# Pairs of lots of 512 tokens instead of 416, seven plain chunks instead of eight, and ten operand buffers

## The chip, the core and the metric

The kernel runs on one core of one Trainium2 chip. The metric is device time in microseconds (us). In the views PE is the matmul engine (PEld its weight loads), DVE the vector engine, ACT the scalar engine, POOL the GpSimd engine and SP the engine that issues most DMAs. Each engine works through its own instructions in the order in which they were issued; semaphores order the engines against each other.

## The reference

The input is `x` of 8 batches, 3008 tokens, 256 channels: 24064 tokens in all. Two stages follow each other.

```
X = np.fft.rfft(x, axis=1)
Yr = Xr @ w_r - Xi @ w_i + b_r
Yi = Xr @ w_i + Xi @ w_r + b_i
Yr, Yi = soft threshold by 0.01
y = np.fft.irfft(Yr + 1j * Yi, n=3008, axis=1)
...
gate = 1.0 / (1.0 + np.exp(-(y @ w_gate)))
out = (gate * (y @ w_val)) @ w_out
```

`w_gate` and `w_val` are 256 x 1536, `w_out` is 1536 x 256. In the kernel the 1536 hidden channels are NF = 12 blocks of 128.

## The kernel before

**The transform stage.** The Fourier transform is made of matmuls with tables. `fwd_a` or `half_a` make its first factor and store to DRAM (`zd`), `fwd_b` the second, `mix` the products with `w_r` and `w_i`, `inv_b` and `inv_a` the way back (through `vd` in DRAM). Batches 0 and 1 are done nearly alone; batches 2 to 7 run as side work beside the plain chunks.

**Numbers in two parts.** A product of single precision is made of three matmuls: the operand is split in a high part (`hh`, `xh`, a cast on ACT) and a low part (`hl`, `xl`, a subtraction on DVE or POOL), and high x high, high x low and low x high are added in PSUM.

**Plain chunks.** The first NPL = 8 chunks of CW = 512 tokens go through `ffn1` and `ffn2`: for each of 12 blocks 12 matmuls of the first layer and 6 of the second, each of 512 columns, 216 matmuls a chunk. The side work is spread over the units of chunks 1 to 7 by weights. `SIDE_GAP` = 14 units at the end of the last chunk have none; there POOL, ACT and DVE also make sums of weights (`make_t`, `make_t1`) and the operands of the first pair.

**Pairs of lots.** The other 19968 tokens go in NPR = 24 pairs of two lots of HW = 416 tokens. A pair is a 2 x 2 block product in Winograd's form: seven products in place of eight. It has 12 half-steps, called e = 0 to 11 here, in `half(k, extra)` with k = 12 p + e for pair p. A half-step issues to PE: four products (banks a, b, d, c; operands a11, s2, s3, s1; 12 matmuls), then `second` (the output layer for an earlier block, 12 matmuls), then three products (bank a with operand a12, bank c with s4, bank d with a22; 9 matmuls). These are 33 matmuls of HW columns, 396 a pair. DVE adds the banks up (u, v, c12, tags `u`, `v`, `c`), ACT does sigmoids and high parts, DVE and POOL low parts. Even half-steps make gates, odd ones the products with them. The order is written out by hand here (`tc.manual_schedule()`): an engine's instructions run in the order of the code. Three lists hold what a half-step leaves to the next: `before_sums`, `after_m1` (run behind the first copy) and `before_second`. Through them, at the start of an even half-step, ACT makes the high parts of u and c12 and POOL the low part of c12.

**Operands.** `operand(p, name, sub_)` makes one of a pair's seven operands from the pair's tokens (`ypair`, loaded by `load_y`): for s1, s2, s3 and s4 a sum or difference on POOL, then for all a high part on ACT and a low part on POOL. The results lie in tiles of tag `xop`, NCB = 12 of them. In half-step e of pair p `extra()` makes those operands of pair p + 1 whose entry in `PREP_AT` is e; the call stands just ahead of `second`. `PREP` is (a11, s1, s2, s3, a12, s4, a22), `PREP_AT` (1, 3, 5, 7, 8, 11, 11).

**Outputs.** In half-step e = 2 `second` ends the pair before: four copies from PSUM to `ot` tiles (two on ACT, two on DVE, `bufs=4`), each followed by a store from SP.

Of the kernel before, what the change touches and what calls it, by code (L numbers as in the profile page):

```python
# [9 lines left out]
F32 = mybir.dt.float32  # L10
# [11 lines left out]
NQ = 2 * NK2  # L22
LAM = float(np.float32(0.01))
GROUPS = (1, 1, 2, 2, 2)
CW = 512
NPL = 8
HW = 416
FFT_BANKS, L1_BANKS, L2_BANKS = 3, 3, 2

NF2K, NR2K, NLD, NST, NBIG, NME, NVF, NHH, NSG, NYF = 5, 5, 3, 3, 5, 2, 3, 3, 2, 2  # L30
NCB, NTMP, NHP = 12, 9, 12

SIDE_GAP = 14
PRE = 4
# [2 lines left out]
NCONV = 6  # L37
# [69 lines left out]
def tile_fft_mix_ffn(ctx: ExitStack, tc, x, w_r, w_i, b_r, b_i, w_one, w_out, mf, mi, mis, fa, fa32, fb, out):  # L107
    nc = tc.nc
    B, S, D = x.shape
    P = 128  # L110
    CT = D // P
# [4 lines left out]
    UT = 2 * PT  # L116
    NU = B * H // 2
    T0 = NPL * CW
    NPR = (B * S - T0) // (2 * HW)
    assert T0 + NPR * 2 * HW == B * S  # L120
    NH = NF // 2
# [41 lines left out]
    def load_a(b, h):  # L163
        xf = p0.tile([P, 4, D], F32, name="xf0", bufs=R1 // 8) if b == 0 else big("xf")
        for lo_, hi_ in ((0, 64), (64, 2 * R2)):
            nc.sync.dma_start(xf[lo_:hi_], xv[b, lo_:hi_, 4 * h:4 * h + 4])
        held["x", b, h] = xf

    def product_a(xi, az, whole, copy):

        pa = bank("pa")[:2 * NQ]
        if whole:
            nc.tensor.matmul(pa, fa32_sb, xi, start=True, stop=True)
        else:
            xh = r2k("xh")[:2 * R2]
            xl = r2k("xl")[:2 * R2]
            nc.scalar.copy(xh, xi)
            nc.gpsimd.tensor_sub(xl, xi, xh)
            nc.tensor.matmul(pa, fa_sb[:, 0], xh, start=True, stop=False)
            nc.tensor.matmul(pa, fa_sb[:, 0], xl, start=False, stop=False)  # L180
            nc.tensor.matmul(pa, fa_sb[:, 1], xh, start=False, stop=True)
        copy(az, pa.rearrange("p (h c) -> p h c", h=2))

    def fwd_a(b, h, whole=False):
        xf = held.pop(("x", b, h))
        az = (p0.tile([P, 4, D], F32, name="az0", bufs=3) if b == 0 else big("az"))[:2 * NQ]
        for i in range(2):
            product_a(xf[:2 * R2, 2 * i:2 * i + 2], az[:, 2 * i:2 * i + 2], whole,
                      nc.vector.tensor_copy if b == 0 and i else nc.scalar.copy)
        nc.sync.dma_start(zv[b][:, 4 * h:4 * h + 4], az)  # L190
# [7 lines left out]
    def half_a(b, h, whole):  # L198

        xi = held.pop(("xh", b, h))[:2 * R2]  # L200
        az = p2.tile([P, 2, D], F32, tag="st", bufs=NST, name="azh")[:2 * NQ]
        product_a(xi, az, whole, nc.scalar.copy)
        nc.sync.dma_start(zv[b][:, 2 * h:2 * h + 2], az)


# [104 lines left out]


    def load_v(u):
        vf = p3.tile([P, 2, D], F32, name="vf", bufs=NVF)[:2 * NQ]
        b, h = divmod(2 * u, H)
        nc.sync.dma_start(vf, vv[b][:, h:h + 2])
        held["v", u] = vf
# [10 lines left out]
    def inv_a(u):  # L327
        vf = held.pop(("v", u))
        pa = bank("pia")[:, :CT * UT].rearrange("p (c h k) -> p c h k", c=CT, h=2)
        for hh in range(2):  # L330
            for ct in range(CT):
                nc.tensor.matmul(pa[:, ct, hh], vf[:, hh, ct * P:(ct + 1) * P], fb_sb[:, :PT], start=True, stop=True)  # L332
        py = pa.rearrange("p c h k -> p c (h k)")
        lo = u * UT
        n = 0
        if lo < T0:
            c, at = divmod(lo, CW)
            n = min(UT, CW - at)
            split_y(c, at, n, py[:, :, :n])
        if n == UT:  # L340
            return
        if lo + n < T0:
            t = p3.tile([P, CT, UT], F32, name="carry", bufs=1)[:, :, :UT - n]
            nc.scalar.copy(t, py[:, :, n:])
            held["carry", c + 1] = t, UT - n
        else:
            t = p3.tile([P, CT, UT], F32, name="yf", bufs=NYF)[:, :, :UT - n]
            nc.scalar.copy(t, py[:, :, n:])
            nc.sync.dma_start(yd[:, :, lo + n - T0:lo + UT - T0], t)

# [125 lines left out]

    def sums(fp, i):
        f0, f1 = 2 * fp, 2 * fp + 1
        b = p4.tile([P, 2, CT, P], F32, name="tb", bufs=1)
        nc.gpsimd.tensor_add(b, w1h[:, f0:f0 + 2, i], w1l[:, f0:f0 + 2, i])  # L480
        return b

    def make_t(fp, i):

        b = sums(fp, i)
        t = p4.tile([P, 3, P], F32, name="tt", bufs=1)
        g = nc.gpsimd
        g.tensor_sub(t[:, 1], b[:, 1, 1], b[:, 1, 0])
        g.tensor_add(t[:, 0], t[:, 1], b[:, 0, 0])
        g.tensor_sub(t[:, 2], b[:, 0, 1], t[:, 0])  # L490
        nc.scalar.copy(th[:, fp, i], t)
        sub(tl[:, fp, i], t, th[:, fp, i])

    def make_t1(fp, i):
        f0, f1 = 2 * fp, 2 * fp + 1
        b = p4.tile([P, 2, P], F32, name="tb1", bufs=1)
        nc.gpsimd.tensor_add(b, w1h[:, f0:f0 + 2, i, 0], w1l[:, f0:f0 + 2, i, 0])
        nc.gpsimd.tensor_sub(b[:, 1], b[:, 1], b[:, 0])
        nc.scalar.copy(w1h[:, f1, i, 0], b[:, 1])
        sub(w1l[:, f1, i, 0], b[:, 1], w1h[:, f1, i, 0])  # L500
# [39 lines left out]
        xs[p][name] = t  # L540

    PREP = ("a11", "s1", "s2", "s3", "a12", "s4", "a22")
    PREP_AT = (1, 3, 5, 7, 8, 11, 11)

    def tmp(name):
        return p5.tile([P, HW], F32, tag="tmp", bufs=NTMP, name=name)
# [17 lines left out]
    def second(n, j):  # L564

        if not 0 <= n < NPR * NH:
            return
        p, fp = divmod(n, NH)
        f = 2 * fp + j
        if f == 0:  # L570
            po[p] = [[bank("po", "l2", L2_BANKS)[:, :HW] for _ in range(CT)],
                     [psg.tile([P, 512], F32, tag="po2", bufs=CT, name="po2")[:, :HW] for _ in range(CT)]]
        for s in range(2):
            hh, hl = hq.pop((n, j, s))
            for ct in range(CT):
                o = po[p][s][ct]
                wh, wl = (w2[:, f, v, ct * P:(ct + 1) * P] for v in range(2))
                nc.tensor.matmul(o, wh, hh, start=(f == 0), stop=False)  # L578
                nc.tensor.matmul(o, wl, hh, start=False, stop=False)  # L579
                nc.tensor.matmul(o, wh, hl, start=False, stop=(f == NF - 1))  # L580
        if f == NF - 1:
            for s, os in enumerate(po.pop(p)):
                for ct, o in enumerate(os):
                    ot = p5.tile([P, HW], F32, name="ot2", bufs=4)
                    (nc.scalar.copy if ct == 0 else nc.vector.tensor_copy)(ot, o)  # L585
                    at = T0 + (2 * p + s) * HW
                    nc.sync.dma_start(out[ct * P:(ct + 1) * P, at:at + HW], ot)
# [20 lines left out]
    def half(k, extra):  # L608
# [32 lines left out]
            high(n, 1, 1, v)  # L641
            low(n, 1, 1, v, sub)
        run(before_second)
        if extra:
            extra()
        second(n - 1 - (i == 0), 1 - i)
        product(a, "a12", "b21", more=True)
        if i == 0:
# [94 lines left out]
    def load_part():  # L743
        k, f = parts.pop(0)
        raws.append((k, f, raw_words(w_out[f // 2] if k else w_one[f])))

    def convert():
        k, f, raw = raws.pop(0)
        if k:
            from_f64(raw, w2[:, f:f + 2, 0], w2[:, f:f + 2, 1])  # L750
        else:
            from_f64(raw, *(w[:, f].rearrange("p i t n -> p i (t n)") for w in (w1h, w1l)))
# [12 lines left out]
    na = R1 // 8  # L765
# [10 lines left out]
        fwd_a(1, h, True)  # L776
    for i, (_, u) in enumerate(first):
        u()
        if i < NCONV:
            load_part()  # L780
        if 0 <= i - 1 < NCONV:
            convert()
        if i == len(first) - 3:
            load_part()
            load_part()
        if i >= len(first) - 2:
            load_a(1, na - len(first) - 2 + i)
    p0s.close()
    p3 = p3s.enter_context(tc.tile_pool(name="p3", bufs=2, side="right", reuse_waits="tile"))
    for u in own0:  # L790
        load_v(u)
    for h in range(EARLY // 2, na):
        if h < EARLY // 2 + 2:
            convert()
        fwd_a(1, h, True)
        if h + 2 < na:
            load_a(1, h + 2)
    load_part()
    load_part()
    beside = [(b, h) for b in groups[2] for h in range(R1 // 4)]  # L800
    for bh in beside[:2]:
# [85 lines left out]
    with tc.manual_schedule():  # L887
        for k in range(2 * NPR * NH):
            p, e = divmod(k, 2 * NH)
            extra = None  # L890
            if p + 1 < NPR:
                if e == 0:
                    load_y(p + 1)
                def extra(p=p, e=e):
                    for name, at in zip(PREP, PREP_AT):
                        if at == e:
                            operand(p + 1, name, nc.gpsimd.tensor_sub)
            half(k, extra)
        for todo in before_sums, after_m1, before_second:
            run(todo)  # L900
        n = NPR * NH
        second(n - 2, 1)
        second(n - 1, 0)
        second(n - 1, 1)
# [29 lines left out]
```

## Time and profile before

| | us |
|---|---|
| median of 3 runs | 2941.66 (2939.41 to 2949.0) |
| the profiled execution | 2936.81 |
| its span | 2935.0 |
| first matmul of a pair | at about 1104 of the span |
| one pair of lots, 12 half-steps | about 75.8 |

The span is from the first to the last instruction; the profiled execution's time is 1.8 us longer than it. The page counts 15736 matmuls in all. A matmul's duration on the page is modelled and overlaps the next one's, so the pace of PE is read from the start of one matmul to the start of the next. Up to about 226 us transforms and the first chunk run with gaps; from there to about 1065 plain chunks run beside the side work; from 1104 on there are only pairs.

### The profile page before, as it was taken

How to read it: one execution, taken by the hardware profiler on the slowest of the kernel's cores; microseconds unless marked ns; L12 is line 12 of the kernel's file. 1: busy time of each engine (PE TensorE's matmuls, PEld its weight loads, DVE VectorE, ACT ScalarE, POOL GpSimd, SP SyncE). 2: the span in 40 equal slices, each digit the busy share in tenths (PEclk: the TensorE clock that was granted, in tenths of full speed). 3: DMA queues.
4: the chain of work that ended last, by engine and by line, in shares of the span. 5: the costliest groups of instructions: out<-in, count | busy, mean ns of one | idle time of the engine just before them, and what ended most of it. 6: DMA issues, size and time to landing. Idle time of an engine off the chain costs nothing.

```text
span 2935.0 us, 43626 instructions
## 1 busy us (share of the span) xinstructions
PE 2853.9 (97%) x15736; PEld 2645.7 (90%) x15736; DVE 2231.4 (76%) x3607; ACT 1384.2 (47%) x2667; POOL 856.3 (29%) x786
## 2 busy tenths in 40 slices
PE   8889999999999899999999999999999999999999
PEld 5657898798789788999999999999999999999999
DVE  5566896298279537888888888888888888888887
ACT  4455455555655344444444444444444444444443
POOL 1251002300400513333333333333333333333331
PEclk9899999999999999999999999999999999999999
DMA  8646545674665430000000000000000000000000
GB/s 268 189 134 190 145 136 142 193 215 129 180 188 162 136 113 8 24 24 24 24 24 24 24 24 24 24 24 24 24 24 24 24 24 24 24 16 21 24 13 24
DMA packets 174041, 226.23 MB, mean 77 GB/s; under 512 B 15458, under 2 KB 135840, under 8 KB 173824
## 3 DMA queue, kind: packets, MB, share of 16 engines
q1 hardware_dynamic: 160560, 210.74, 23.6%
q0 software_dynamic: 13168, 12.66, 1.9%
q8 instruction: 124, 2.03, 0.3%
q14 instruction: 93, 0.76, 0.1%
q10 hardware_dynamic: 96, 0.04, 0.0%
HBM read 127.95 MB, written 95.42 MB: 76 GB/s over the span
## 4 chain that ended last, share of the span: by engine, by line
PE 61%; DVE 10%; issue 2%; POOL 1%; DMA 1%; ACT 0%; DVEq 0%; SPq 0%; POOLq 0%; ACTq 0%
PE pd L600 10%; PE pc L600 10%; PE pa L600 10%; PE po L580 7%; PE po L579 7%; PE po L578 7%; PE pb L600 5%; DVE hl L562 2%; PE pia L332 1%; DVE u L661 1%; DVE c L655 1%; DVE ot L585 1%; DVE ys L271 1%; DVE v L632 1%; DVE xsl L247 0%
## 5 line engine op out<-in xcount | busy, mean ns | idle before, releaser
L580 PE MATMUL po<-hl,w 128*128 128x416 f32 x1152 | 406.8, 353 | 0.0
L579 PE MATMUL po<-hh,w 128*128 128x416 f32 x1152 | 405.8, 352 | 0.0
L578 PE MATMUL po<-hh,w 128*128 128x416 f32 x1152 | 405.1, 352 | 0.0
L600 PE MATMUL pc<-s,w1h 128*128 128x416 f32 x1152 | 311.7, 352 | 2.6 <-DVE v L634 2.6
L600 PE MATMUL pa<-a,w1h 128*128 128x416 f32 x1152 | 310.8, 351 | 0.4 <-ACT u L626 0.4
L558 ACT CAST hh<-v 128x416 fp32r<-128x416 f32 x144 | 77.8, 540 | 335.6 <-DVE v L640 335.6
L659 POOL TENSOR_TENSOR c<-c,c 128x416 f32<-128x416 f32 x144 | 157.0, 1090 | 247.0 <-DVE c L655 246.9
L630 DVE TENSOR_TENSOR u<-u,pb 128x416 f32<-128x416 f32 x288 | 167.4, 581 | 72.6 <-PE pb L600 60.5
L562 POOL TENSOR_TENSOR hl<-c,hh 128x416 fp32r<-128x416 f32 x144 | 156.2, 1084 | 221.0 <-ACT hh L558 221.0
L600 PEld LDWEIGHTS pc<-s,w1h 128*128 128x128 f32 x1152 | 215.4, 188 | 5.5 <-DVE v L634 3.6
L600 PEld LDWEIGHTS pa<-a,w1h 128*128 128x128 f32 x1152 | 215.8, 188 | 3.9 <-ACT u L626 0.8
L580 PEld LDWEIGHTS po<-hl,w 128*128 128x128 f32 x1152 | 216.8, 188 | 2.5
L578 PEld LDWEIGHTS po<-hh,w 128*128 128x128 f32 x1152 | 217.2, 189 | 1.8
L579 PEld LDWEIGHTS po<-hh,w 128*128 128x128 f32 x1152 | 216.1, 188 | 2.1
L372 DVE TENSOR_TENSOR sg<-sg,pv 128x512 f32<-128x512 f32 x96 | 65.9, 686 | 183.1 <-PE pv L368 170.2
L600 PE MATMUL pa<-a,w1l 128*128 128x416 f32 x576 | 200.5, 348 | 0.0
L600 PE MATMUL pc<-s,w1l 128*128 128x416 f32 x576 | 199.6, 346 | 0.0
L539 POOL TENSOR_TENSOR s<-sop,s 128x416 fp32r<-128x416 f32 x69 | 74.9, 1086 | 426.0 <-ACT s L538 419.9
L655 DVE TENSOR_TENSOR c<-u,pc 128x416 f32<-128x416 f32 x288 | 168.6, 585 | 37.3 <-PE pc L600 29.8
L632 DVE TENSOR_TENSOR v<-u,pd 128x416 f32<-128x416 f32 x288 | 169.3, 588 | 30.7 <-PE pc L600 0.9
L634 DVE TENSOR_TENSOR v<-v,pc 128x416 f32<-128x416 f32 x288 | 169.1, 587 | 31.0 <-DVE v L632 1.4
L661 DVE TENSOR_TENSOR u<-u,pd 128x416 f32<-128x416 f32 x288 | 169.2, 588 | 30.7 <-DVE c L655 0.9
(175 smaller groups left out, 7442.5 us busy)
## 6 DMA issues: line engine op xcount, KB each, us to landing
zf<-zd SPq DMA_DIRECT2D x96, 256.0 KB, 3.6
vd<-vz SPq DMA_DIRECT2D x96, 256.0 KB, 2.9
vf<-vd SPq DMA_DIRECT2D x128, 192.0 KB, 3.5
ypair<-yd SPq DMA_DIRECT2D x24, 832.0 KB, 4.5
out_dram<-ot SPq DMA_DIRECT2D x96, 208.0 KB, 2.1
yd<-yf SPq DMA_DIRECT2D x106, 188.0 KB, 3.2
zd<-az SPq DMA_DIRECT2D x48, 384.0 KB, 3.7
xf<-in_x_dram SPq DMA_DIRECT2D x48, 256.0 KB, 4.4
```

The lines of the kernel that those rows point to most:

```text
L558: nc.scalar.copy(hq[n, j, s][0], h)
L562: sub_(hl, h, hh)
L578: nc.tensor.matmul(o, wh, hh, start=(f == 0), stop=False)
L579: nc.tensor.matmul(o, wl, hh, start=False, stop=False)
L580: nc.tensor.matmul(o, wh, hl, start=False, stop=(f == NF - 1))
L600: nc.tensor.matmul(o, l, r, start=not more and l is wh and r is xh, stop=l is wl, skip_group_check=more)
L630: add(u, u, b)
L632: add(v, u, d)
L634: add(v, v, c)
L655: add(c12, u, c)
L659: nc.gpsimd.tensor_mul(c12, g12, c12)
L661: add(u, u, d)
```

## The change

- HW from 416 to 512 and NPL from 8 to 7: 3584 tokens in plain chunks, 20480 in 20 pairs of 1024 tokens.
- NCB from 12 to 10, and `PREP_AT` to (2, 4, 6, 11, 11, 12, 12). An entry of 12 means half-step 0 of the pair itself: s4 and a22 are made in the half-step that is the first to use them. `load_y` moves from e = 0 to e = 1.
- The copies of the outputs have three `ot2` tiles in place of four.
- Tiles of `make_t` and `make_t1` share buffers with the tiles `vf` and `yf` of `inv_a`.
- `half_a` makes its low part on DVE in place of POOL.
- Some loads at the end of the first two batches' transforms are issued in another order: those of `x` for batch 1 earlier, those of raw weights one unit later at first and then spread over the loop.

```diff
-NPL = 8
-HW = 416
+NPL = 7
+HW = 512
-NCB, NTMP, NHP = 12, 9, 12
+NCB, NTMP, NHP = 10, 9, 12
...
-    def product_a(xi, az, whole, copy):
+    def product_a(xi, az, whole, copy, sub_=nc.gpsimd.tensor_sub):
...
-            nc.gpsimd.tensor_sub(xl, xi, xh)
+            sub_(xl, xi, xh)
...
-        product_a(xi, az, whole, nc.scalar.copy)
+        product_a(xi, az, whole, nc.scalar.copy, sub)
...
-        vf = p3.tile([P, 2, D], F32, name="vf", bufs=NVF)[:2 * NQ]
+        vf = p3.tile([P, 2, D], F32, tag="vf", bufs=NVF, name="vf")[:2 * NQ]
...
-            t = p3.tile([P, CT, UT], F32, name="yf", bufs=NYF)[:, :, :UT - n]
+            t = p3.tile([P, 3, P], F32, tag="yf", bufs=NYF, name="yf").rearrange("p a b -> p (a b)")
+            t = t[:, :CT * (UT - n)].rearrange("p (c k) -> p c k", c=CT)
...
-        b = p4.tile([P, 2, CT, P], F32, name="tb", bufs=1)
+        b = p3.tile([P, 2, CT, P], F32, tag="vf", bufs=NVF, name="tb")
...
-        t = p4.tile([P, 3, P], F32, name="tt", bufs=1)
+        t = p3.tile([P, 3, P], F32, tag="yf", bufs=NYF, name="tt")
...
-        b = p4.tile([P, 2, P], F32, name="tb1", bufs=1)
+        b = p3.tile([P, 3, P], F32, tag="yf", bufs=NYF, name="tb1")[:, :2]
...
-    PREP_AT = (1, 3, 5, 7, 8, 11, 11)
+    PREP_AT = (2, 4, 6, 11, 11, 12, 12)
...
-                    ot = p5.tile([P, HW], F32, name="ot2", bufs=4)
+                    ot = p5.tile([P, HW], F32, name="ot2", bufs=3)
...
-        if i < NCONV:
+        if 1 <= i <= NCONV:
             load_part()
-        if 0 <= i - 1 < NCONV:
+        if 2 <= i < NCONV + 2:
             convert()
         if i == len(first) - 3:
             load_part()
-            load_part()
-        if i >= len(first) - 2:
-            load_a(1, na - len(first) - 2 + i)
+        if i >= len(first) - 3:
+            load_a(1, na - len(first) - 1 + i)
...
+    load_a(1, na - 1)
...
         if h < EARLY // 2 + 2:
             convert()
+            load_part()
         fwd_a(1, h, True)
-        if h + 2 < na:
-            load_a(1, h + 2)
-    load_part()
     load_part()
...
-            extra = None
-            if p + 1 < NPR:
-                if e == 0:
-                    load_y(p + 1)
-                def extra(p=p, e=e):
-                    for name, at in zip(PREP, PREP_AT):
-                        if at == e:
-                            operand(p + 1, name, nc.gpsimd.tensor_sub)
+            if e == 1 and p + 1 < NPR:
+                load_y(p + 1)
+
+            def extra(p=p, e=e):
+                for name, at in zip(PREP, PREP_AT):
+                    q, when = p + 1 - at // (2 * NH), at % (2 * NH)
+                    if when == e and 0 < q < NPR:
+                        operand(q, name, nc.gpsimd.tensor_sub)
+
             half(k, extra)
```

More of the change, by code (lines that the diff above doesn't have):

```diff
@@ L643, in half @@
         run(before_second)
-        if extra:
-            extra()
+        extra()
         second(n - 1 - (i == 0), 1 - i)
```

## The prediction

> **What bounds the kernel now.** First the page's head, for the whole:
>
> ```profile
> span 2935.0 us, 43626 instructions
> ...
> PE 2853.9 (97%) x15736; PEld 2645.7 (90%) x15736; DVE 2231.4 (76%) x3607; ACT 1384.2 (47%) x2667; POOL 856.3 (29%) x786
> ```
>
> PE is the bound on average, but an average over unlike stages. So next the view by windows, cut at the stages. Its columns are the stretch, its length, the busy us and count of PE, PEld, DVE, ACT and POOL, and the granted clock.
>
> ```profile
> core 0: us, PE busy (x) PEld busy (x) DVE busy (x) ACT busy (x) POOL busy (x), PEclk, DMA share, GB/s
> 226.00:460.00 234.00, 230.02 (x1529) 203.32 (x1529) 199.16 (x375) 120.27 (x202) 20.11 (x25) 0.99 0.55 155
> 845.00:980.00 135.00, 132.52 (x977) 123.12 (x977) 126.17 (x238) 71.63 (x124) 13.68 (x17) 1.00 0.55 159
> 980.00:1065.00 85.00, 77.08 (x428) 65.02 (x427) 30.57 (x40) 33.56 (x74) 35.26 (x51) 0.92 0.61 177
> 1128.00:2932.00 1804.00, 1790.20 (x9419) 1748.92 (x9417) 1494.44 (x2327) 808.37 (x1632) 609.13 (x537) 1.00 0.07 22
> ```
>
> Beside the side work PE is busy 98% of the time and DVE 85 to 93%: two bounds close together. From 1128 us on, in the pairs, it is PE at 99% with DVE at 83%. There the pace of PE decides; it is read from the timeline between two starts:
>
> ```profile
> 1071.64 0.39 PE L385 MATMUL po<-hh,w 128*128 128x512 f32 x1
> ...
> 1101.09 0.39 PE L385 MATMUL po<-hh,w 128*128 128x512 f32 x1
> ...
> 1340.32 0.35 PE L578 MATMUL po<-hh,w 128*128 128x416 f32 x1
> ...
> 1346.57 0.35 PE L578 MATMUL po<-hh,w 128*128 128x416 f32 x1
> ...
> 1351.51 0.35 PE L600 MATMUL pb<-s,tl 128*128 128x416 f32 x1
> 1352.46 0.65 PE L600 MATMUL pd<-s,th 128*128 128x416 f32 x2 [0.60 <-DVE u L661]
> ```
>
> The first two are seven units of a plain chunk apart: 126 matmuls of 512 columns in 29.45 us, 233.7 ns each. The next two are one half-step apart: 33 matmuls of 416 columns in 6.25 us, 189.4 ns each. Per column that is 0.456 and 0.455 ns: a matmul costs its columns and nothing more. The last two show the one stall that each pair has: 0.95 us from start to start at bank d, where 0.19 would do, 0.76 us lost.
>
> **The change part by part.**
>
> *The matmuls.* Before: 24 x 396 = 9504 of 189.4 ns, 1800.1 us. After: 20 x 396 = 7920 of 512 columns at 233.7 ns, 1850.9 us. One plain chunk less is 216 x 233.7 ns = 50.5 us. The net is +0.3 us; at 0.455 ns a column throughout it would be -4. I take 0. The form with seven products saves 9216 columns, and fewer, wider matmuls save nothing that these rows show. The Trainium skill, "TensorE: Matmul & The Clock Gate", section "Wait — 56ns, not 53.3ns?", gives a warm matmul N / 2.4 GHz and about 2.5 ns fixed; by it 1800 matmuls fewer and 9216 columns fewer would save an estimated 8.3 us, against 0 to 4 by the rows, whose pace is 8% slower than the page's for either width.
>
> *What of the chunk's 50.5 us is got back.* The side work stays and is packed into 12 units fewer. Where PE bounds, all comes back. Where DVE bounds, only the chunk's DVE work does: two instructions a unit (L372 and L376 in the rows below, 0.69 and 0.81 us), 12 x 1.5 = 18 us. DVE is at 85 to 93% against PE's 98%, nearer to the first: I take 45 of 50.5, **+5** (0 to +32).
>
> *Operands in the pair's own first half-step.* This is the costly part. Durations that change with the width, from the groups of instructions (count, busy us, mean ns):
>
> ```profile
> L178 POOL TENSOR_TENSOR xl<-xf,xh 94x512 fp32r<-94x512 f32 x64 | 82.7, 1305 | 95.0 <-ACT yf L348 43.3 <-PE pa L180 31.3 <-ACT xh L177 7.6
> L536 POOL TENSOR_TENSOR sop<-ypair,sop 128x416 f32<-128x416 f32 x24 | 34.2, 1424 | 1.3 <-DVE s L539 1.3
> L375 ACT CAST hh<-sg 128x512 fp32r<-128x512 f32 x96 | 59.6, 620 | 62.6 <-DVE sg L372 62.1
> L372 DVE TENSOR_TENSOR sg<-sg,pv 128x512 f32<-128x512 f32 x96 | 65.9, 686 | 183.1 <-PE pv L368 170.2 <-ACT az L182 6.4 <-ACT xh L177 5.1
> L376 DVE TENSOR_TENSOR hl<-sg,hh 128x512 fp32r<-128x512 f32 x96 | 77.7, 810 | 38.5 <-ACT hh L375 37.7
> L661 DVE TENSOR_TENSOR u<-u,pd 128x416 f32<-128x416 f32 x288 | 169.2, 588 | 30.7 <-DVE c L655 0.9
> ```
>
> So at 512 a POOL subtraction takes 1.31 us, an ACT cast 0.62, a DVE addition 0.69. The difference for s4 (L536) takes 1.42 at 416; at 512 it is 1.64 (with the 0.22 us that a subtraction gains) to 1.75 (in proportion). Now the timeline of a half-step 0 before the change; it starts at 1331.78:
>
> ```profile
> 1331.78 0.54 PE L600 MATMUL pa<-a,w1h 128*128 128x416 f32 x2
> 1336.92 0.54 PE L600 MATMUL pc<-s,w1h 128*128 128x416 f32 x2
> 1338.05 0.54 PE L600 MATMUL pa<-a,w1h 128*128 128x416 f32 x2
> ...
> 1332.18 0.59 DVE L661 TENSOR_TENSOR u<-u,pd 128x416 f32<-128x416 f32 x1
> 1332.80 1.50 DVE L666 TENSOR_TENSOR u<-u 128x416 f32<-128x416 f32 x1
> ...
> 1334.34 0.54 ACT L558 CAST hh<-u 128x416 fp32r<-128x416 f32 x1 [1.23 <-DVE u L666]
> 1334.78 0.54 ACT L558 CAST hh<-c 128x416 fp32r<-128x416 f32 x1
> ...
> 1332.77 1.09 POOL L659 TENSOR_TENSOR c<-c,c 128x416 f32<-128x416 f32 x1
> 1335.40 1.08 POOL L562 TENSOR_TENSOR hl<-c,hh 128x416 fp32r<-128x416 f32 x1 [1.54 <-ACT hh L558]
> ```
>
> POOL's low part of c12 ends 4.70 us into the half-step: it hangs on DVE's two steps on u (the second 1.50 us beside a busy POOL) and ACT's two casts. In the new order POOL does, behind it, the difference for s4, its low part, then the low part of a22. At 512, from the half-step's start: u at 0.4 + 0.73, the product to about 2.95 (1.50 x 512/416), the casts' two starts to 3.5, the low part of c12 from 4.1 to 5.4; the difference to 7.1; ACT's high part of s4 to 7.75; POOL's low part of s4 to 9.1 and of a22 to 10.45. PE gets to bank c after 27 matmuls, 6.3 us. It starts s4's high part at 7.8 (1.5 late), its low part at 9.2, two matmuls on a22, whose low part is there at 10.5, and ends at 11.0 where 33 x 0.2337 = 7.7 was due: 3.3 us. With the uncontended product of u and the shorter difference it is 2.3, with every step in proportion and later casts 3.6. I take 3.0, for the 19 pairs behind the first: **+57** (44 to 68). Behind these instructions on ACT stands the sigmoid of bank a, which the next half-step needs, but by 9 us it is done. s3 and a12 move into e = 11, where two operands were made before; POOL's extra instruction there delays the product on c12 by about a microsecond, and that ends (at 2 us) before the casts above need it: 0. Their buffers are those of a11 and s1, last read by the half-step's first 12 matmuls: 0. The load at e = 1 waits for these reads on SP, where nothing is queued that a half-step waits for, and has till e = 2: 0.
>
> *Three output tiles.* The fourth copy takes the tile of the first, once that has been stored.
>
> ```profile
> 1348.64 0.90 ACT L585 COPY ot<-po 128x416 f32<-128x416 f32 x2
> 1350.14 1.07 DVE L585 COPY ot<-po 128x416 f32<-128x416 f32 x2
> 1351.82 0.59 DVE L661 TENSOR_TENSOR u<-u,pd 128x416 f32<-128x416 f32 x1
> ...
> out_dram<-ot SPq DMA_DIRECT2D x96, 208.0 KB, 2.1
> ```
>
> This is e = 2 (from 1344.30): DVE's copies push u, which frees bank d, and that is the old stall. After, ACT's v comes at 4.15 us, a11's high part (now in this half-step) at 4.7, the first copy ends at 5.9; its store of 256 KB needs 2.1 x 256/208 = 2.6 at most, 2.1 at least: the tile is free at 8.0 to 8.5. DVE, which adds from 2.0 to 4.1 in three steps of 0.69, then makes two low parts beside POOL (to 6.6) and one copy (to 7.3), waits; copy, c and u follow to 10.3, and bank d, due at 39 x 0.2337 = 9.1, starts at about 10.4: 1.3 us (0.9 to 1.9), 25 us in 19 pairs, against 23 x 0.76 = 17.5 before: **+7** (0 to +19). Without the wait it would be 0.25 a pair, as DVE grows by 688/588 = 1.17 and PE by 1.23.
>
> *The clock.* Windows of 3.41 us:
>
> ```profile
> 330.70:334.11 3.41, 1.59 (x14) 1.57 (x14) 2.29 (x6) 0.96 (x3) 0.00 (x0) 1.00 0.39 118
> 334.11:337.52 3.41, 3.41 (x19) 3.41 (x18) 1.56 (x2) 1.92 (x4) 0.00 (x0) 0.50 0.66 165
> ...
> 1108.94:1112.35 3.41, 2.10 (x12) 2.07 (x12) 2.31 (x5) 1.56 (x4) 0.00 (x0) 1.00 0.29 109
> 1112.35:1115.76 3.41, 2.98 (x16) 2.58 (x15) 2.41 (x5) 1.10 (x3) 0.00 (x0) 1.00 0.00 0
> ```
>
> Behind a window with PE busy for 1.59 us the clock was 0.50; behind one with 2.10 it stayed. In the stall above, from 6.3 to 9.7, PE is busy for about 1.0 by the same measure. A window at half clock costs up to 1.7 us, part of it inside the wait: 1.2 us, in two pairs of three: **+15** (0 to 27).
>
> *The early loads, and the shared tiles.*
>
> ```profile
> PE pa L173 <- DMA xf<-in_x_dram: 7.0, 1, 7.0
> PEld pa L180 <- POOL xl L178: 23.4, 23, 2.7
> POOL tt L488 <- DVE tl L492: 24.7, 11, 19.1
> ```
>
> The one wait for `x` can go by the earlier load (7 us), and a few of the waits for POOL's `xl` by DVE (0.69 in place of 1.31): **-8** (-18 to +4; raw weights come later in places). A second `tt` lets POOL run ahead; but it takes turns with `yf`, whose tile is free only after a store, in a stretch where PE already loses 8 of 85 us: **+3** (-10 to +20).
>
> *Sum:* 0 + 5 + 57 + 7 + 15 - 8 + 3 = +79 on the profiled execution's 2936.8 (the span and 1.8), 3016. The runs' median lies 4.9 above that execution; I add 2: **3018**.
>
> **The rivals.** *The operands come in time* (faster). If POOL's chain ends by 6.3 us of half-step 0, bank c waits for nothing, the clock stays, and DVE's better ratio leaves 0.25 us of the old 0.76 a pair: 5 - 12.5 - 8 + 3 gives 2924. For it: POOL is busy a third of the time. Against: it isn't load but latency, and the chain is 2.8 us too long by rows. Chance 0.12. *Part of it:* a stall of about 1 us and no fall of the clock, 2937 to 2950: 0.07. *The clock stays up* in these stalls: 3003, chance 0.25, and it lies among the slower ones. The Trainium skill, "TensorE: Matmul & The Clock Gate", section "What's actually happening", has the clock halved after at least one idle window of about 3.4 us. By that rule a window with some matmuls is safe; the row at 330.70 with 14 matmuls speaks against it. *DVE takes over beside the side work:* 27 us more, 3045: 0.10.
>
> **How the numbers follow.** Forecast with its own spread (the clock either way) 0.71, DVE 0.10, part 0.07, in time 0.12. Faster by over 0.3% (about what a measurement here can tell from no change) is the first rival, 0.12; within 0.3% most of the second, 0.06; slower 0.82. The range, 2947 to 3045, leaves out the first two rivals' times but for the edge, and what lies above the DVE case. The slower cases' own range is 2975 to 3045.
>
> **What would show it.** A pair takes 33 x 12 x 0.2337 = 92.5 us of matmuls and about 5 more. Right: in e = 0 PE idles at bank c on ACT's and POOL's s4, twice, then on a22; DVE's second `ot` copy waits for a store; windows of PEclk under 1.00 through the pairs; the first pair begins some 50 us earlier. Wrong: pairs of 93 us, or POOL's s4 ahead of 6 us; matmuls of 512 at under 230 ns; or a first pair at over 1085 us.

## The result, and the profile after

| | before | after |
|---|---|---|
| median of 4 runs, us | 2942.66 (2939.41 to 2949.0) | 3016.1 (3014.5 to 3024.96) |
| ratio, with its 95% interval | | 1.0253 (1.0227 to 1.0279) |
| the profiled execution, us | 2936.81 | 3015.88 |
| first matmul of the first pair, us of the span | 1103.9 | 1070.75 |
| from there to the last matmul, us | 1827.1 | 1938.1 |

The change makes the kernel 2.5% slower. Between the profiled executions lie 79.1 us. The pairs begin 33.1 us earlier, since a chunk is gone, and take 111.0 us longer. For matmuls alone the prediction moved 50.8 us from the one side to the other (1850.9 less 1800.1). So both sides show a loss: the first part gives back 17 us less than the chunk's 50.5, and the pairs grow by 60 us more than the extra columns ask for.

The page's head after the change, and last the shares of the chain of work that ended last:

```profile
span 3014.1 us, 38905 instructions
PE 2871.0 (95%) x13936; PEld 2335.5 (77%) x13936; DVE 2206.0 (73%) x3203; ACT 1348.0 (45%) x2364; POOL 837.9 (28%) x678
PE 69%; DVE 16%; POOL 5%; DMA 3%; issue 3%; ACT 3%; DVEq 0%; SPq 0%; ACTq 0%; POOLq 0%
```

PE lost 1800 matmuls and is still busy for 17 us longer, at 95% of the span in place of 97%. A head like this can't say why. The view by windows, with the columns of the prediction's, cut at the stages of the new kernel:

```profile
226.00:470.00 244.00, 239.48 (x1621) 212.24 (x1620) 212.46 (x403) 126.24 (x214) 22.75 (x29) 0.99 0.57 159
1030.00:1071.00 41.00, 31.58 (x110) 24.12 (x111) 20.29 (x32) 14.15 (x32) 27.32 (x43) 0.80 0.01 3
1095.00:3008.00 1913.00, 1843.60 (x7843) 1477.18 (x7842) 1480.73 (x1937) 784.94 (x1355) 605.84 (x446) 0.99 0.06 21
```

Beside the side work little is new: PE 98%, DVE 87% (85% before). The last 41 us before the pairs are worse than the stretch that stood there before (91%, 0.92): PE at 77%, the clock at 0.80, and POOL busy for 27 of 41 us, making sums of weights. In the pairs PE went from 99% to 96% (1843.6 of 1913.0), DVE from 83% to 77%: no engine became the bound, PE waits.

Where it waits stands in PE's timeline. First a half-step e = 0, from 1356.12 to 1366.85 (columns: start, us, instruction; in brackets the idle time before it and what ended it):

```profile
1356.12 0.61 PE L601 MATMUL pa<-a,w1h 128*128 128x512 f32 x2
...
1363.70 0.50 PE L601 MATMUL pc<-s,w1h 128*128 128x512 f32 x1 [1.17 <-ACT s L539]
...
1365.05 0.50 PE L601 MATMUL pc<-s,w1h 128*128 128x512 f32 x1 [0.84 <-POOL s L540]
...
1366.29 0.49 PE L601 MATMUL pd<-a,th 128*128 128x512 f32 x1 [0.27 <-POOL a L540]
...
1366.85 0.63 PE L601 MATMUL pa<-a,w1h 128*128 128x512 f32 x2
...
1374.50 0.61 PE L601 MATMUL pa<-a,w1h 128*128 128x512 f32 x2
...
1377.22 0.40 PE L579 MATMUL po<-hh,w 128*128 128x512 f32 x1
...
1380.04 0.63 PE L601 MATMUL pa<-a,w1h 128*128 128x512 f32 x2
...
1382.12 0.61 PE L601 MATMUL pa<-a,w1h 128*128 128x512 f32 x2
...
1385.04 0.73 PE L601 MATMUL pd<-s,th 128*128 128x512 f32 x2 [1.40 <-DVE u L661]
```

The rows from 1374.50 on are the half-step e = 2. Its 33 matmuls end without a gap at 1382.12: 7.62 us. So e = 0, which has as many, lost 10.73 - 7.62 = 3.11 us, in three stops: bank c waits for the high part of s4 (ACT), again for its low part (POOL), and bank d for the low part of a22 (POOL). The last row is the stall at bank d: 6 matmuls after 1382.12 it was due at 1383.5 and starts 1.5 us late.

The same half-step e = 0 on POOL, the engine that is late:

```profile
1360.02 1.29 POOL L563 TENSOR_TENSOR hl<-c,hh 128x512 fp32r<-128x512 f32 x1 [1.80 <-ACT hh L559]
1361.27 1.73 POOL L537 TENSOR_TENSOR sop<-ypair,sop 128x512 f32<-128x512 f32 x1
1363.73 1.27 POOL L540 TENSOR_TENSOR s<-sop,s 128x512 fp32r<-128x512 f32 x1 [0.73 <-ACT s L539]
1364.95 1.28 POOL L540 TENSOR_TENSOR a<-ypair,a 128x512 fp32r<-128x512 f32 x1
```

Four subtractions in a row, with one wait for ACT's cast between them: POOL starts the first 3.9 us into the half-step, when ACT has made the high part of c12, and ends the last at 1366.23, 10.1 us into it. Over the whole span POOL is busy for 28%. An engine busy for little more than a quarter of the time, placed behind one late start, makes the largest loss of the pairs.

### The profile page after: what moved, and what is told of

Its sections match the earlier page's. It is cut to its first block, busy times and chain, and to the rows that moved or that the text cites. A ratio compares the mean times of both kernels' runs of the same rounds, so it can differ in the third digit from the quotient of the medians.

```text
span 3014.1 us, 38905 instructions
## 1 busy us (share of the span) xinstructions
PE 2871.0 (95%) x13936; PEld 2335.5 (77%) x13936; DVE 2206.0 (73%) x3203; ACT 1348.0 (45%) x2364; POOL 837.9 (28%) x678
## 4 chain that ended last, share of the span: by engine, by line
PE 69%; DVE 16%; POOL 5%; DMA 3%; issue 3%; ACT 3%; DVEq 0%; SPq 0%; ACTq 0%; POOLq 0%
PE pd L601 9%; PE pa L601 9%; PE pc L601 8%; PE po L581 6%; PE po L580 6%; PE po L579 6%; PE pb L601 4%; PE pia L332 3%; PE pm L264 2%; DVE ys L271 1%; DVE u L661 1%; PE pb L230 1%; DMA out_dram<-ot 1%; DVE u L666 1%; DVE c L655 1%
## 5 line engine op out<-in xcount | busy, mean ns | idle before, releaser
L581 PE MATMUL po<-hl,w 128*128 128x512 f32 x960 | 381.5, 397 | 0.0
L580 PE MATMUL po<-hh,w 128*128 128x512 f32 x960 | 380.6, 396 | 0.0
L579 PE MATMUL po<-hh,w 128*128 128x512 f32 x960 | 379.9, 396 | 0.0
L601 PE MATMUL pc<-s,w1h 128*128 128x512 f32 x960 | 306.5, 397 | 41.1 <-ACT s L539 22.2
L601 PE MATMUL pa<-a,w1h 128*128 128x512 f32 x960 | 302.6, 397 | 0.5 <-ACT u L627 0.5
L601 PEld LDWEIGHTS pc<-s,w1h 128*128 128x128 f32 x960 | 179.8, 188 | 94.5 <-ACT s L539 30.4
L661 DVE TENSOR_TENSOR u<-u,pd 128x512 f32<-128x512 f32 x240 | 165.0, 688 | 36.3 <-PE pd L601 12.6
L264 PE MATMUL pm<-w_sb,xsh 128*128 128x256 f32 x1008 | 190.4, 288 | 1.1 <-ACT xsf L242 0.7
L601 PE MATMUL pa<-a,w1l 128*128 128x512 f32 x480 | 188.1, 392 | 0.0
L601 PE MATMUL pc<-s,w1l 128*128 128x512 f32 x480 | 187.3, 390 | 0.0
L633 DVE TENSOR_TENSOR v<-u,pd 128x512 f32<-128x512 f32 x240 | 165.1, 688 | 25.9 <-PE pc L601 0.5
L635 DVE TENSOR_TENSOR v<-v,pc 128x512 f32<-128x512 f32 x240 | 164.9, 687 | 25.6 <-DVE v L633 0.9
```

The source lines that it names most:

```text
L264: nc.tensor.matmul(o, l, r, start=(i == 0), stop=(i == len(mms) - 1))
L601: nc.tensor.matmul(o, l, r, start=not more and l is wh and r is xh, stop=l is wl, skip_group_check=more)
L633: add(v, u, d)
L635: add(v, v, c)
L661: add(u, u, d)
```

## The experiments

Each time comes from a set of runs on one chip, in which the kernel before ran too; it took 2938.9 to 2941.1 there. The change itself, 3015.88, was not run again in these sets. "Pairs" is the time from the first pair's first matmul to the last matmul; "start of the pairs" is that first matmul's place in the span. Runs with one time have one execution, the profiled one; for the others the last two columns are those of their profiled execution.

| what is changed | time, us | start of the pairs | pairs |
|---|---|---|---|
| before: operands late | 3001.37 | 1105.2 | 1890.4 |
| before: three output tiles | 2965.43 | 1112.3 | 1846.3 |
| before: shared tiles | 2947.14 | 1113.3 | 1827.8 |
| before: early loads | 2927.85 (10 runs) | 1092.0 | 1828.2 |
| after: s4's difference early, low parts on DVE | 2963.98 | 1078.7 | 1878.3 |
| after: low parts on DVE alone | 2977.7 | 1069.1 | 1901.6 |
| after: four output tiles | 2992.18 | 1070.0 | 1915.8 |
| after: sums on another tile | 3027.08 | 1082.9 | 1937.3 |
| after: sums wholly apart | 3000.45 | 1056.3 | 1937.2 |
| after: operands and outputs mended | 2927.31 (4 runs) | 1083.3 | 1847.4 |
| after: sums apart as well | 2912.78 (6 runs) | 1067.9 | 1847.0 |

The theory was that the late operands cost most of it, by POOL's latency. Its rivals were the width itself (fewer, wider matmuls), the outputs' tiles, and the first part of the kernel. The first four edits do one part of the change each on the kernel before, at 416 tokens.

### Operands in the pair's own first half-step, at 416

```diff
-NCB, NTMP, NHP = 12, 9, 12
+NCB, NTMP, NHP = 10, 9, 12
...
-    PREP_AT = (1, 3, 5, 7, 8, 11, 11)
+    PREP_AT = (2, 4, 6, 11, 11, 12, 12)
```

with `load_y` at e = 1 and the new `extra()`.

> The kernel before with the operand part of the change alone: ten buffers, the new places, the load at half-step 1; lots stay at 416. Theory (latency of POOL's chain in half-step 0): each of 23 pair boundaries shows two gaps of PE at bank c (high part of s4, then low part) and one at bank d, together 2.3 to 2.7 us, worked out with 416 columns; with some windows of half clock 2990 to 3015 us. Rival (the wait comes from the width of 512): no gaps at bank c, 2935 to 2950 us.

Measured: 3001.37 against 2941.11, and the pairs 63 us longer. Its timeline of PE at one e = 0:

```profile
1347.53 0.46 PE L600 MATMUL pc<-s,w1h 128*128 128x416 f32 x1 [1.32 <-ACT s L538]
...
1348.67 0.46 PE L600 MATMUL pc<-s,w1h 128*128 128x416 f32 x1 [0.69 <-POOL s L539]
...
1349.70 0.46 PE L600 MATMUL pd<-a,th 128*128 128x416 f32 x1 [0.20 <-POOL a L539]
```

The same three stops at the same three operands, with the old width. From start to start they are 1.67, 1.14 and 0.55 us in place of 0.19 each. The whole half-step takes 9.36 us in most of the 23 pairs, 6.27 before: a loss of 3.1 a pair, a little more than expected, since the first matmul behind a stop is slower too (0.29 us to the next start in place of 0.19). The view of PE's waits (us in total, times, longest) shows what went in exchange:

```profile
PE pc L600 <- ACT s L538: 29.9, 23, 1.3
PE pc L600 <- POOL s L539: 16.0, 23, 0.8
...
PE pd L600 <- DVE u L661: 0.4, 1, 0.4
```

In the trace before, that last line was:

```profile
PE pd L600 <- DVE u L661: 14.2, 24, 0.8
```

So the old wait at bank d is gone. At e = 2 DVE's low part of u takes 0.58 us here; before, beside POOL's difference for s1 (1348.35 in that trace), it took 1.47. The two copies behind it are as long as before (1.08 and 1.07 together). The stops lose 23 x 3.1 = 71, the half-step e = 3 gives back 18 (6.29 us in the mean in place of 7.08), and of the 63 some 10 are left for the 10 windows at half clock that this run's pairs have. The width isn't needed for the loss.

### Three output tiles, at 416

```diff
-                    ot = p5.tile([P, HW], F32, name="ot2", bufs=4)
+                    ot = p5.tile([P, HW], F32, name="ot2", bufs=3)
```

> The kernel before with three output tiles in place of four, nothing else. Theory: the fourth copy waits for the first store (the copy ends 4.9 us into half-step 2, the store lands 2.1 us later, DVE is there at 6.3), and the gap at bank d of half-step 3 grows from 0.76 to about 1.4 us: 23 x 0.65, about +15 us, 2950 to 2960 us. Rival (the store is back in time, the longer gap after the change comes from the copy of a11 or the width): within 3 us of before.

Measured: 2965.43 against 2941.11, above the 2950 to 2960 expected. Against the trace before it is 28.6 us more, of which only 19.2 lie in the pairs; about 8 us lie ahead of them, where the edit does nothing. There the windows at half clock that begin in the first 130 us sum to 58 us, against 30.7 in the trace before; one execution can differ by so much. In the view of PE's waits:

```profile
PE pd L600 <- DVE u L661: 30.3, 25, 2.1
```

That is 14.2 before. The half-step e = 3, in which this bank is due, takes 7.86 us in the mean in place of 7.08: 17.9 us over 23 pairs. Of these 2.4 are one pair's that ran into a window at half clock, and the rest is about the 15 that were expected of the fourth copy's wait for a store.

### Tiles of the sums shared with inv_a, at 416

```diff
-        b = p4.tile([P, 2, CT, P], F32, name="tb", bufs=1)
+        b = p3.tile([P, 2, CT, P], F32, tag="vf", bufs=NVF, name="tb")
...
-        t = p4.tile([P, 3, P], F32, name="tt", bufs=1)
+        t = p3.tile([P, 3, P], F32, tag="yf", bufs=NYF, name="tt")
...
-        b = p4.tile([P, 2, P], F32, name="tb1", bufs=1)
+        b = p3.tile([P, 3, P], F32, tag="yf", bufs=NYF, name="tb1")[:, :2]
```

> The kernel before with the tiles of the weights' sums shared with vf and yf, nothing else. Theory: the sums queue behind the transforms' tiles, come after the side work, and ACT, in order, holds the sigmoids of the plain chunk behind their casts: PE loses 12 to 20 us between the last transform and the first pair, 2950 to 2965 us. Rival (the loss there comes from packing the side work into 12 units fewer): within 4 us of before.

Measured: 2947.14 against 2941.11, less than the 2950 to 2965 expected. The place is the one expected: from the last matmul of `inv_a` to the first pair it takes 54.2 us, 42.2 before, and the pairs are unchanged (1827.8). But `inv_a` ends earlier in its chunk here: from the first matmul of the seventh chunk to the first pair it is 200.2 us in place of 194.6. So the price at 416 is about 6 us by one execution of each, not much above the rival's 4. In that stretch PE now waits for a plain chunk's gate, which stands on ACT behind the casts of sums:

```profile
PE pv L367 <- ACT sg L371: 8.9, 2, 5.6
```

The kernel before has no such wait there.

### Early loads, at 416

The edit is the change's block of loads and `half_a` with its low part on DVE, put in the kernel before. It ran once and then again with ten runs.

> The kernel before with the order of the loads and the low part on DVE in the half blocks of the transform alone. Theory: the first plain chunk ends some 11 us earlier (second chunk's first matmul at 215 in place of 226 us) and all of it stays to the end, as PE bounds from there: 2928 to 2934 us. Rival (it is given back beside the side work, where DVE is near its bound): the second chunk begins earlier and the first pair doesn't, 2938 to 2943 us.

> The kernel before with the order of the loads and the low part on DVE alone, timed in rounds: 2926 to 2932 us, 0.3 to 0.5% faster than before.

Measured: 2926.82, and 2927.85 against 2938.94 in the repeat, ratio 0.9960 (0.9946 to 0.9973). In the first run the second chunk begins at 215.7 in place of 226.3 and the pairs 11.3 us earlier. This part of the change is a gain, slightly above the prediction's 8.

### The operands mended, in the changed kernel

Next come repairs of the changed kernel, one cost at a time. First the difference for s4, made at e = 8 of the pair before in the buffer that it has anyway, and the low parts of s4 and a22 on DVE in place of POOL.

```diff
-    g.tensor_sub(v, a12, v)
...
-        operand(q, name, nc.gpsimd.tensor_sub)
+        operand(q, name, sub if at == 12 else nc.gpsimd.tensor_sub)
+    if e == 8 and p + 1 < NPR:
+        s4_difference(p + 1)
```

> The changed kernel with the difference for s4 made on POOL in half-step 8 (it needs no operand buffer), and the low parts of s4 and a22 on DVE in place of POOL; casts stay in half-step 0. Theory: the casts come at 5.6 to 6.8 us, the low parts to 7.5; the three gaps of together 2.9 us shrink to about 0.5, no window of half clock in the pairs: 19 x 2.4 = 46 and 14 for the clock, 2955 to 2965 us. Rival (DVE or the buffers set the wait): gaps of over 2 us stay, 3000 us or more.

Then the same without the early difference: the low parts on DVE alone.

> The changed kernel with only the low parts of s4 and a22 on DVE in half-step 0; the difference for s4 stays there on POOL. Theory: the first gap at bank c (1.3 us net, up to ACT's cast of s4 behind POOL's difference) stays, the second (1.1) falls to about 0.4 and the one at a22 goes: 2.9 to 1.8 us, 19 x 1.1 = 21 and part of the clock, 2985 to 2995 us. Rival (ACT's cast is late by ACT's own queue, not by the difference): the first gap changes too.

Measured: 2963.98 and 2977.7, against 3015.88 for the change. In the first, PE's waits and one row of its timeline:

```profile
PE pd L605 <- DVE u L665: 25.9, 20, 1.7
...
PE pc L605 <- DVE s L540: 6.3, 18, 0.4
```

```profile
1363.64 0.50 PE L605 MATMUL pc<-s,w1h 128*128 128x512 f32 x1 [0.35 <-DVE s L540]
```

Of the three stops one is left, 0.35 us of idle time, and no window of the pairs is at half clock. The pairs take 59.8 us less (1938.1 to 1878.3): e = 0 takes 8.27 us in place of 10.73, which is 47 us in 19 pairs; the 12.5 of the clock make up the rest to within 1 us. The 8 us by which the pairs start later here than in the change aren't of the edit. The second chunk already begins at 220.5 in place of 215.3: the clock was at half for 27.3 us from 19.0 on, in the change for 13.7 from 29.6.

With the low parts alone the first stop stays, since the difference for s4 is still POOL's, and the other two shrink:

```profile
1356.95 0.50 PE L601 MATMUL pc<-s,w1h 128*128 128x512 f32 x1 [1.16 <-ACT s L539]
...
1357.67 0.50 PE L601 MATMUL pc<-s,w1h 128*128 128x512 f32 x1 [0.22 <-DVE s L540]
```

That is 2977.7, below the 2985 to 2995 that were expected: the stop at a22 is gone too, and with a loss of 1.95 us in place of 3.11 (e = 0 takes 9.57) no window of the pairs is at half clock. The expectation had counted the gaps and left the clock as it was.

### Four output tiles, at 512

```diff
-NCB, NTMP, NHP = 10, 9, 12
+NCB, NTMP, NHP = 10, 8, 12
...
-                    ot = p5.tile([P, HW], F32, name="ot2", bufs=3)
+                    ot = p5.tile([P, HW], F32, name="ot2", bufs=4)
```

> The changed kernel with four output tiles again; to make room the temporaries of the first layer (tag tmp) are eight in place of nine. Theory: the fourth copy no longer waits for a store and the gap at bank d of half-step 3 falls from 1.5 to about 0.3 us: 19 x 1.2, 2990 to 2998 us, with the gaps at bank c as they are. Rival (DVE is late there by itself, by the cast of a11 and wider copies): the gap stays above 1 us, 3010 us or more. If eight temporaries are too few, gaps appear in other half-steps.

Measured: 2992.18, as expected, with the stall at bank d gone: e = 3 takes 7.61 us, where it took 9.28 in the mean, and e = 4 to 11 take 7.61 to 7.62 in the mean, so eight temporaries are enough. The stall had lost 31.6 us, yet the pairs gain 22.3 (1938.1 to 1915.8). The windows of this run, cut on the grid of the granted clock, around e = 0 of two pairs that follow each other:

```profile
1358.45:1361.86 3.41, 1.37 (x6) 0.67 (x4) 1.26 (x1) 1.63 (x3) 2.68 (x3) 1.00 0.00 0
1361.86:1365.27 3.41, 3.30 (x9) 2.25 (x8) 1.38 (x2) 0.91 (x2) 0.54 (x1) 0.50 0.50 135
...
1454.02:1457.43 3.41, 1.38 (x6) 0.58 (x5) 1.50 (x1) 1.63 (x3) 2.68 (x3) 1.00 0.02 5
1457.43:1460.84 3.41, 3.41 (x9) 2.30 (x8) 1.38 (x2) 0.68 (x2) 0.77 (x1) 0.50 0.43 105
```

Every pair now has a window at half clock, 19 of them in place of 8. The windows at half clock lie 95.57 us apart, and the pairs settle at that length from 96.1 at first; by the change's pair without such a window (96.18 us) less the stall of 1.7 it would be 94.5. So the clock takes back about 1.1 us a pair.

### The sums apart

Two runs took the sums off the shared tiles. The first gives `tt` the tile of `carry` and `tb1` one of its own, and leaves `tb` on `vf`; in the second `tt` and `tb1` take the tile of `carry`, and `tb` leaves `vf` too, for the plain chunk's output tiles. The lines of `tt`, and of `tb` in the second:

```diff
-        t = p3.tile([P, 3, P], F32, tag="yf", bufs=NYF, name="tt")
+        t = p3.tile([P, 3, P], F32, tag="carry", bufs=1, name="tt")
```

```diff
-        b = p3.tile([P, 2, CT, P], F32, tag="vf", bufs=NVF, name="tb")
+        b = p3.tile([P, 2, CT, P], F32, tag="ot", bufs=2, name="tb")
```

> The changed kernel with the second tile of the weights' sums (tt) in the place of the chunk carry tile, and tb1 a tile of its own, so that neither takes turns with yf; tb still shares with vf. Theory: the sums come beside the side work again and PE loses 10 to 15 us less ahead of the first pair, which begins at 1055 to 1062 us in place of 1070.8; 3000 to 3006 us. Rival (tb behind vf holds them back just as well, or the packing does): the first pair at 1068 us or later, 3012 us or more.

> The changed kernel with all three tiles of the weights' sums away from vf and yf: tb in the place of the plain chunks' output tiles, tt and tb1 in that of the chunk carry. Theory after the run with tt alone (where POOL's first sum waited 18 to 20 us for a matmul to release a vf tile): it is tb behind vf; now the sums come beside the side work and the first pair begins at 1050 to 1060 us in place of 1070.8; 2996 to 3006 us. Rival (the packing of the side work into 12 units fewer): 1068 us or later, 3012 us or more.

The first fell: 3027.08, with the pairs starting at 1082.9, 12 us later than in the change. POOL's waits from 940 us to its first pair say what held the sums:

```profile
POOL tb L482 <- PE pia L332: 72.5, 4, 32.1
```

`tb` takes its turn on `vf` with the loads of `inv_a`, so POOL stands until PE has read them, and a private tile behind it changes nothing of that. In the changed kernel the same wait is 81.1 us in 4 times. The second run holds: 3000.45, the pairs start at 1056.3, 14.5 us earlier than in the change. PE's wait for the plain chunk's gate, from 900 us to the first pair, first in the change, then in this run:

```profile
PE pv L367 <- ACT sg L371: 12.3, 4, 4.4
```

```profile
PE pv L368 <- ACT sg L372: 5.6, 3, 2.5
```

The gate's sigmoid stands on ACT among the casts of sums, and ACT waits for POOL's sums in the change (from 1010 to 1071 us):

```profile
ACT th L492 <- POOL tt L491: 12.4, 9, 2.8
ACT w1h L500 <- POOL tb L499: 10.9, 7, 2.4
```

So the price is paid through `tb`'s turn on `vf`. From the first matmul of the sixth chunk to the first pair it is 243.4 us in the change, 248.3 in the first run and 231.1 in the second: there the second gains 12.2 of its 14.5. Of the 12 us that the first run is late, 7.2 lie ahead of that chunk, before any sum is made; why is not settled.

### The mends together

Last, the changed kernel with the operands and the output tiles mended, and then with the sums apart too.

> The changed kernel with the two mended parts of the pairs together: the difference for s4 in half-step 8 and the low parts of s4 and a22 on DVE; four output tiles with eight temporaries. Theory: gaps of 0.5 us at bank c and 0.3 at bank d remain, no half clock; pairs take 20 x 91.5 + 19 x 0.8 + 7 = 1852 us behind a first pair at 1071: 2925 to 2938 us, just below the kernel before. Rival (the parts collide on DVE, or pairs of this length fall into step with the clock's windows): 2945 us or more.

> All three mends together on the changed kernel: the operands of half-step 0, four output tiles, the sums' tiles apart from vf and yf. Theory: the three gains add up, as they lie in different stretches: the first pair at 1056 to 1060 us, 1848 us of pairs, 2908 to 2918 us, about 1% below the kernel before and about 0.5% below either mended version alone. Rival (the sums' time is given back in the pairs, or the other way): 2922 us or more.

Measured: 2927.31 (2923.81 to 2937.06) against 2938.94, ratio 0.9952 (0.9935 to 0.9969); with the sums apart 2912.78 (2911.02 to 2924.1) against 2940.58, ratio 0.9906 (0.9885 to 0.9927). Both lie where they were expected. The last is the fastest of all (the profiled one of its six executions took 2921.48, and the start of the pairs above is that one's). From the sixth chunk to the first pair the sums apart bring 11.6 us here (246.4 to 234.8), much as in the change. The pairs of this last kernel by windows, and the wait that is left there:

```profile
1080.00:2910.00 1830.00, 1820.92 (x7864) 1474.99 (x7864) 1515.58 (x1989) 789.12 (x1365) 561.34 (x410) 1.00 0.06 22
```

```profile
PE pc L606 <- DVE s L541: 6.8, 18, 0.4
```

PE is busy 99.5% of the time, at full clock. With the stops gone the wider pairs hold: 1847.0 us for 20480 tokens is 0.0902 us a token, against 1827.1 for 19968, 0.0915. Not all of the 0.9% is theirs, though: the early loads alone, on the kernel before, gave 0.4%.

## Why the prediction was right, step by step

The forecast of 3018 stands 1.9 us above the median, and its sum, +79, is what the profiled executions differ by. But that it came out so close is luck: four terms were well off, in both directions.

| term | predicted | measured |
|---|---|---|
| matmuls | 0 | -21 |
| the chunk's time not given back | +5 | +14 |
| operands in e = 0 | +57 | +59 |
| three output tiles | +7 | +12.5 |
| clock | +15 | +12.5 |
| early loads | -8 | -11 |
| shared tiles | +3 | +14.5 |
| sum | +79 | +80.5 |

The 1.4 us by which the measured terms exceed 79.1 are within what such readings overlap; the chunk's term is a remainder, and so makes the part ahead of the pairs come out by itself.

**The operands.** Right, and by the steps given. From the half-step's start the prediction had the low part of c12 ready at 5.4, the difference at 7.1, bank c at 7.8 and 9.2, the low part of a22 at 10.45 and the end at 11.0; the rows give 5.2, 6.9, 7.6, 8.9, 10.1 and 10.7. Everything came a quarter of a microsecond sooner, and since the matmuls did too (7.62 in place of 7.7), the loss stayed: 3.1 a pair where 3.3 came out by the steps and 3.0 was taken. What carried it were durations of the same operations in the trace before, scaled by a row that exists at 512. The run at 416 shows that the order alone makes these stops, with no more work on POOL. The two mended runs differ only in when POOL makes the difference for s4: made earlier, still on POOL, it takes the first stop away. So it is POOL's latency at this place, not its load.

**The matmuls.** The step that failed is "a matmul costs its columns and nothing more". The 233.7 ns for 512 columns came from units of a plain chunk, a mixture of layers. The rows of e = 2 above give 12 matmuls of the first layer in 2.72 us (227 ns), 12 of the output layer in 2.82 (235 ns), 9 of the first layer in 2.08 (231 ns): a mean of 230.9. Two rows of the same kind before the change, the first of the output layer and the first behind it:

```profile
1334.06 0.35 PE L578 MATMUL po<-hh,w 128*128 128x416 f32 x1
...
1336.35 0.54 PE L600 MATMUL pa<-a,w1h 128*128 128x416 f32 x2
```

There it is 2.29 us for the output layer, and from the half-step's start at 1331.78 2.28 for the first: no difference at 416. So 7920 matmuls take 7920 x 0.2310 = 1829.2, not 1850.9, a gain of 21 us that the form of the kernel does give. The prediction's own sign of being wrong, matmuls at under 230 ns, thus came true for part of them. Why the first layer alone is quicker at 512 stays open. The Trainium skill, "TensorE: Matmul & The Clock Gate", section "Wait — 56ns, not 53.3ns?", has a fixed part for each matmul beside its columns: by it the estimate was a gain of 8.3 us. The sign agrees with this trace, the pace doesn't: the gain is more than twice that.

**The chunk.** The pairs started 33.1 us earlier: the chunk's 50.5 and the loads' 11, less 14.5 for the shared tiles, leave 14 not given back. That is a remainder, and it lies in the bounds of 0 to 32, nearer the middle than the 5 that was taken. The reason that the prediction gave, DVE as a second bound beside the side work, is not what the traces show: from the second chunk to the first pair PE's waits for DVE come to 4.6 us before and 7.0 after. A wait for one read of `zd` grew more, first before, then after:

```profile
PE pb L230 <- DMA zf<-zd: 1.1, 1, 1.1
```

```profile
PE pb L230 <- DMA zf<-zd: 6.0, 1, 6.0
```

With the sums wholly apart it is 7.8 in 3 times, so it does not hang on them. Windows at half clock in that stretch sum to 17 us before, 48 after and 24 with the sums apart. The read makes 5 of the 14 us; what makes it late has not been tested, so the cause of the 14 stays open.

**The outputs.** The mechanism of the new wait was right, the size about half. The old stall was misread: the prediction gave it to DVE's copies, but the run of the operands at 416 has the same copies and no stall, while DVE's low part of u is 0.9 us quicker there, more than the stall's 0.76. The first tile's reuse shows in DVE's and SP's rows of e = 2:

```profile
1380.38 0.68 DVE L586 COPY ot<-po 128x512 f32<-128x512 f32 x1
1382.90 0.69 DVE L586 COPY ot<-po 128x512 f32<-128x512 f32 x1 [1.85 <-DMA out_dram<-ot]
1384.30 0.69 DVE L661 TENSOR_TENSOR u<-u,pd 128x512 f32<-128x512 f32 x1
```

```profile
1380.68 3.27 SPq L588 DMA_DIRECT2D out_dram<-ot  x4
```

The tile is free 2.2 us after its store was issued, 8.4 us into the half-step (8.0 to 8.5 was predicted), and bank d starts at 10.54 (10.4). But it was due at 39 x 0.231 = 9.0, not 9.1, and e = 3 takes 9.28 us in the mean where 7.61 is due: 1.7 a pair and not 1.3, 31.6 us over the 19 pairs, against 19.0 before (7.08 where 6.25 is due, 23 times). The quicker matmuls made the same stall longer.

**The clock.** Right in kind and near in size. Windows on its grid, at a pair that falls and at the next, that doesn't:

```profile
1265.19:1268.60 3.41, 1.50 (x5) 0.71 (x5) 1.13 (x2) 1.63 (x3) 2.59 (x3) 1.00 0.00 0
1268.60:1272.02 3.42, 3.42 (x8) 2.74 (x9) 0.87 (x2) 1.55 (x3) 0.00 (x0) 0.50 0.68 212
...
1360.76:1364.17 3.41, 2.25 (x9) 1.30 (x7) 2.79 (x3) 1.77 (x4) 2.68 (x3) 1.00 0.00 0
1364.17:1367.59 3.42, 2.30 (x10) 1.57 (x10) 1.23 (x2) 1.13 (x3) 2.06 (x2) 1.00 0.14 24
```

A stop of the same length is 1.50 us of work in the one window and 2.25 in the other (the prediction had about 1.0), by where it falls on the grid. From the last matmul ahead of the first stop (1264.41) to the same one a pair later it took 97.74 us, and to the next one 96.18: 1.56 for a window at half clock, more than the 1.2 taken, in 8 of 19 pairs, fewer than two of three; the two errors nearly cancel. The Trainium skill, "TensorE: Matmul & The Clock Gate", section "What's actually happening", asks for at least one idle window of that length. These rows go further than the page: a window with five matmuls was enough.

**Loads and shared tiles.** The loads gave 11 for 8; PE's waits for the low part of `half_a` fell as said (from 60 to 250 us, 9.4 us for POOL's before and 1.9 for DVE's after). The shared tiles cost 14.5 for 3, within the bounds, but by another tile than the prediction's: it named `yf` and its store, and taking `tt` and `tb1` off `yf` gained nothing; it is `tb`'s turn on `vf`. The row that spoke against them, the stretch in which PE already lost 8 of 85 us, should have weighed more: sums that come late fall together with the last plain chunk's gates on ACT.

**The rivals.** Operands in time and part of it fell with the first timeline. The clock staying up is what the runs with shorter stops show, but the changed kernel isn't among them. DVE taking over beside the side work is not seen: PE's waits for it there grew by 2.4 us, not 27.

## What to carry to other kernels

When work is moved later to save a buffer, add up the latency of its engine from the moment at which it can start, instruction by instruction with durations of the same shape; the engine's load says little (POOL at 28% made the costliest stops here). The same goes for tiles taken in turns: a copy that waits for a store, or side work that waits for a tile of the main path, is late however idle its engine is; mending these three turned 2.5% slower into 0.9% faster. A sum that comes out right is no proof of its terms: here each had to be measured alone.

## What the runs showed of the hardware

- The granted clock is decided on a grid of 3.413 us, as the spacings in the next point give it. In the quoted windows a window with PE busy for 1.37 to 1.59 us is followed by one at 0.50, one with 2.10 or 2.25 by one at 1.00. Busy time by this measure gives no sharp limit: in the changed kernel 1.94 us (at 2330.15) was followed by 0.50 and 1.75 (at 2350.57) by 1.00.
- A kernel of equal periods can lock to that grid. With four output tiles the windows at half clock came every 95.57 us, exactly 28 windows, and every pair was hit; in the changed kernel, at 290.13 us for three pairs (85 windows) and 194.56 for two (57), every second or third was, from the second hit on. So a shorter stall can give back part of what it saves (22.3 us of 31.6 were kept), and a mend that leaves no window at half clock can gain more than its own gap (36.5 us of the pairs by the low parts on DVE, 22 of them by shorter stops).
- The pace of a matmul of 512 columns was 227 to 235 ns by its place in the half-step, while at 416 both layers ran at 190.
